# Fused attention and two experts on one Trainium2 core: the reciprocal of a slot's sums ahead of the low halves, and the value products in groups of three

## The chip, the cores and the metric

The kernel runs on one core of a Trainium2 chip. The metric is the device time of one execution in microseconds (us), here the median of three runs.

## What is computed

Attention with a local window and a few global columns, and then two experts, all in float32:

```python
scores = 0.125 * q @ k.T + bias        # kept: column < 8, or 0 <= row - column < 96
a = exp(scores - max(scores))
a = a / (sum(a) + 1e-9)
x = a @ v                               # 4 x 8 heads, 768 rows, 64 columns each
x = ((x @ w1) * (x @ w2)) @ w3 @ w_out  # 3072 rows; 512 -> 1024 -> 1024 -> 512
h = x @ w_in                            # 512 -> 2048
out = (h * cos(h)) @ w_out2             # 2048 -> 512
```

`w3 @ w_out` is formed once, as W.

## The kernel before, in words

The attention is cut into 96 units (`NU`). A unit is 128 rows of one pair of heads; three units (`TPB`) make 384 rows of one pair, and four pairs make a block of 384 rows (`UPB` = 12 units, `NB1` = 8 blocks). A unit passes these steps, each a small function:

- `a_scores`: the products of q and k on TensorE, into `s_ps`.
- `a_max` (L584): VectorE adds the bias and takes each row's maximum, `top`.
- `a_exp` (L595): ScalarE's exponential, one instruction for each of two heads, with the row's sum into `st`.
- `a_norm`: VectorE adds 1e-9 to the sums (L605) and takes the reciprocal (L608); then the 128 x 232 exponentials are scaled by it, on ScalarE (L614) or on GpSimd (L616).
- `a_transpose` and `a_tcopy`: TensorE turns the scaled exponentials into `pt_ps` (L623, L625), ScalarE copies them to `pt` (L633, L638).
- `a_values` (L650): products with v into `x_ps`, one bank for three units.
- `a_out`, after the third unit: ScalarE casts `x_ps` to the high half of `xT` (L664), and VectorE subtracts to get the low half (L665).

Large products use three passes over float32 operands that are split in a high and a low half. From unit 22 on q and k are split as well: `a_split_hi` (L522, ScalarE) and `a_split_lo`, two subtractions on VectorE, `kl` (L529) for k's low halves and `hh` (L532) for q's.

The program has three stages. Each engine works through its own queue in the order in which the code is written; nothing reorders it.

1. **Chunks** (the loop over `chunks`, c = 0 to 15; about 9 to 91 us). Chunk c does a sixteenth of W = w3 @ w_out on TensorE, four products `wmm(0)` to `wmm(3)` (L875). Beside these stand steps of the first 14 units: with n = c - 1, chunk c does the maxima and exponentials of unit n, the scaling of n - 1, the transposes of n - 2 and the value products of n - 3. Between them `decode` takes the next steps of decoding the weights from 64-bit words (ScalarE L343, L344, L406; VectorE L348, L352, L360, L410). The bias tables (L480, L481) are made in chunks 0, 3, 6 and 9. Chunk 15 has an order of its own.
2. **Slots** (the double loop over j and i; about 91 to 607 us). Slot `sl` does the scores, maxima and exponentials of unit n = sl + 14, and the transposes of unit n - 1, beside the first expert's products: in slots i = 0 to 7 of a block `up` a and `up` b, in i = 8 to 11 `down`. The value products and `a_out` stand here in groups of six units, in every sixth slot. For sl < 8 the scaling is on ScalarE, later on GpSimd. `up_mult` (L693), `up_hi` (L697) and `up_lo` (L700) form the operand `ab` of `down`.
3. The second expert, from about 610 us on.

The lines around the change in a slot, on VectorE's queue, are `up_lo`, `a_split_lo`, `a_out`, `a_norm`; in a chunk on TensorE's they are `a_values`, `wmm`, `wmm`, `a_transpose`.

Of the kernel before, what the change touches and what calls it, by code (L numbers as in the profile page):

```python
# [25 lines left out]
WIN = 128 + NPV  # L26
# [3 lines left out]
TPB = TB // 128  # L30
UPB = NPAIR * TPB
NU = NB1 * UPB
# [240 lines left out]
def fused(ctx, tc, a_qk, a_v, a_v0, w3p, wo1p, w1p, w2p, winp, wo2p, out):  # L273
# [210 lines left out]
    def where(n):  # L484
        j, r = divmod(n, UPB)
        p, i = divmod(r, TPB)
        return j, p, i, (TPB * j + i) % (S // 128)
# [109 lines left out]
                bias=top[:, n, e:e + 1], scale=-1.0, accum_out=sts[n][:, 0, e:e + 1],  # L597
            )

    def a_norm(n, on_scalar=False, meanwhile=None):  # L600
        if not 0 <= n < NU:
            return
        w = WIN if where(n)[3] else 128
        st = sts.pop(n)
        nc.vector.tensor_scalar(st[:, 1, :], st[:, 0, :], 1e-9, None, ALU.add)  # L605
        if meanwhile:
            meanwhile()
        nc.vector.reciprocal(out=st[:, 1, :], in_=st[:, 1, :])  # L608
        if meanwhile:
            meanwhile()  # L610
        for e in range(2):
            x = es[n][:, e, :w]
            if on_scalar:
                nc.scalar.activation(x, x, ACTF.Copy, scale=st[:, 1, e:e + 1])  # L614
            else:
                nc.gpsimd.tensor_scalar(x, x, st[:, 1, e:e + 1], 1.0, ALU.mult, ALU.mult)  # L616

    def a_transpose(n):
        if not 0 <= n < NU:
            return  # L620
        e_t, t = es.pop(n), where(n)[3]
        for e in range(2):
            nc.tensor.transpose(pt_ps[:, e, 0, :], e_t[:, e, :128], ident)  # L623
            if t:
                nc.tensor.transpose(pt_ps[:NPV, e, 1, :], e_t[:, e, 128:WIN], ident)  # L625
# [14 lines left out]
    def a_values(n):  # L640
        if not 0 <= n < NU:
            return
        j, p, i, t = where(n)
        if i == 0:
            xps[j, p] = p_mm.tile([128, 512], F32, tag="mm", name="x_ps")[:, :TB]
        x, pt, vt = xps[j, p], pts.pop(n), v_raw.pop(n)
        for c in range(2 if t else 1):
            kk = NPV if c else 128
            for e in range(2):
                nc.tensor.matmul(  # L650
                    x[e * 64:(e + 1) * 64, i * 128:(i + 1) * 128],
                    lhsT=vt[:kk, c, e * 64:(e + 1) * 64], rhs=pt[:kk, e, c, :],
                    start=c == 0, stop=c == (1 if t else 0),
                )

    def a_out(n):
        if not 0 <= n < NU:
            return
        j, p, i, _ = where(n)
        if i != TPB - 1:  # L660
            return
        x = xps.pop((j, p))
        t = xT[j, p] = xts.tile([128, 2, TB], F32R, tag="xT", name="xT")
        nc.scalar.copy(out=t[:, 0, :], in_=x)  # L664
        nc.vector.tensor_tensor(  # L665
            out=t[:, 1, :], in0=x, in1=t[:, 0, :].bitcast(F32), op=ALU.subtract
        )
# [88 lines left out]
    with tc.manual_schedule():  # L756
# [81 lines left out]
        def decode(n):  # L838
            for _ in range(n):
                next(steps_left, None)  # L840
# [16 lines left out]
        for i in range(15):  # L857
            decode(1)
            if i == 0:
                a_load_plain(1, False)  # L860
            elif i == 10:
                a_load_plain(2)
            elif i == 12:
                a_load_v(1)
            if i > 6:
                dists = dists or next(steps_b)
        W_ps = {}
        for c, (h, k) in enumerate(chunks):
            n = c - 1
            own = n if n < LEAD else -9  # L870
            if k == 0:
                W_ps = {m: p_mm.tile([128, 512], F32, tag="mm", name="mm") for m in range(4)}

            def wmm(m):
                nc.tensor.matmul(  # L875
                    W_ps[m], lhsT=wt["w3", c][:, m * 128:(m + 1) * 128], rhs=wt["wo1", k],
                    start=k == 0, stop=k == M1 - 1,
                )
                if k == M1 - 1:
                    t = wt["W", 4 * h + m] = wts.tile(  # L880
                        [128, 2, 512], F32R, tag="Wb" if h else "Wa", name="W", bufs=4
                    )
                    nc.scalar.copy(out=t[:, 0, :], in_=W_ps[m])
                    nc.vector.tensor_tensor(  # L884
                        out=t[:, 1, :], in0=W_ps[m], in1=t[:, 0, :].bitcast(F32), op=ALU.subtract
                    )

            a_load(own + 3)
            a_load_v(n - 1 if n > 2 else -1)
            if c % 3 == 0 and c < 12:  # L890
                bias_heads(*dists, range(2 * c // 3, 2 * c // 3 + 2))
            elif c == 10:
                tp.release()
            if n > 0:
                a_scores(own)
            if n > 0:
                a_load_plain(own + 2)
            a_values(n - 3)
            a_max(own)
            if c == 2 * M1 - 1:  # L900
                a_out(n - 3)
                a_norm(n - 1, True)
                for m in range(4):
                    wmm(m)
            decode(1)
            if c < 2 * M1 - 1:
                a_out(n - 3)
            a_split_hi(own + 2)
            a_exp(own)
            a_split_lo(own + 2)  # L910
            if c < 2 * M1 - 1:
                wmm(0)
                wmm(1)
            a_transpose(n - 2)
            a_tcopy(n - 2)
            decode(1)
            if 1 <= n < 2 * M1 - 2:
                a_norm(n - 1, True, lambda: decode(1))
            else:
                decode(2)  # L920
            decode(2 if c < 8 else {14: 1, 15: 2}.get(c, 3))
            if c < 2 * M1 - 1:
                wmm(2)
                wmm(3)
# [72 lines left out]
        for j in range(NB1):  # L997
            for i in range(UPB):
                sl = j * UPB + i
                n = sl + LEAD  # L1000
                last = j == NB1 - 1
                if last and i == 0:
                    attn.release()
                    x2cA = pool("x2cA", 1)
                    late = pool("late", 1)
                    x2_pool.update({k: x2cA for k in ("B11", "T2", "T1", "T3", "B21", "B22")})
                a_load(n + 3)
                if last:
                    if i == 0:
                        x2_loads(0)  # L1010
                    elif i == 1:
                        r0, r1 = stage_tile(), stage_tile()
                        nc.sync.dma_start(out=r0, in_=x2_cols("B12", 0))
                        x2_now = x2_steps(r0, r1)
                    elif 3 <= i < 9:
                        piece_load(0, i - 3)
                a_scores(n)
                a_load_plain(n + 2)
                group = range(n - 1 - GROUP, n - 1) if (n - 1) % GROUP == 0 and n - 2 < NU else ()
                for u in group:  # L1020
                    if u >= LEAD - 2:
                        a_values(u)
                a_load_v(n)
                a_split_hi(n + 2)
                if 1 <= i <= M1:
                    up_mult(j, i - 1)
                    up_hi(j, i - 1)
                a_max(n)
                decode(2 if sl < 14 else 3)
                if i == 0 and j > 0:  # L1030
                    down_out(j - 1, MO - 1)
                    down_store(j - 1, MO - 1)
                elif i > M1:
                    down_out(j, i - M1 - 1)
                    down_store(j, i - M1 - 1)
                if 1 <= i <= M1:
                    up_lo(j, i - 1)
                a_exp(n)
                a_split_lo(n + 2)
                if i < M1:  # L1040
                    up(j, i, "a")
                    up_copy(j, i)
                else:
                    down(j, i - M1, 0)
                for u in group:
                    if u >= LEAD - 2:
                        a_out(u)
                a_transpose(n - 1)
                a_tcopy(n - 1)
                a_norm(n, sl < 8)  # L1050
                decode(2)
                if last and 2 <= i < 10:
                    some(x2_now, 1)
                if i < M1:
                    up(j, i, "b")
                else:
                    down(j, i - M1, 1)
                if last and 2 <= i < 10:
                    some(x2_now, 1)
# [429 lines left out]
```

## Time and profile before

| what | value |
| --- | --- |
| median of three runs | 1076.93 us (1076.87 to 1077.49) |
| the profiled execution's own time | 1076.14 us |
| its span, first to last instruction | 1074.4 us |
| TensorE (PE) busy | 1056.2 us, 98% |
| VectorE (DVE) busy | 830.7 us, 77% |
| ScalarE (ACT) busy | 730.4 us, 68% |
| GpSimd (POOL) busy | 237.8 us, 22% |
| mean granted TensorE clock | 0.998 |

The span is the stretch that the trace covers; the execution's time is 1.7 us longer. A share of busy time is a mean over stages that have different limits, so the prediction reads stretches and not these shares.

### The profile page before, as it was taken

The numbers are of one execution on the slowest core, as the hardware profiler recorded it, in microseconds if no ns is written. First come the engines' busy times: TensorE is split into PE (matmuls) and PEld (weight loads), VectorE is DVE, ScalarE is ACT, GpSimd is POOL, SyncE is SP. The second block draws the span as 40 slices with busy tenths as digits, with TensorE's granted clock in tenths as the row PEclk, the third lists the DMA queues.
The fourth block names the chain that finished last, engine by engine and source line by source line (L and its number), as shares of the span: only waits on it lengthen the run. The fifth ranks groups of instructions, "written<-read, shape, count | busy, mean of one in ns | idle before, by whom it ended". The sixth has DMA issues, their size and how long they took to land.

```text
span 1074.4 us, 17759 instructions
## 1 busy us (share of the span) xinstructions
PE 1056.2 (98%) x5922; PEld 923.5 (86%) x5922; DVE 830.7 (77%) x1812; ACT 730.4 (68%) x1487; POOL 237.8 (22%) x249
## 2 busy tenths in 40 slices
PE   8999999999999999999999999999999999999997
PEld 5446889999999999999999988888888888888886
DVE  8887777878778787887835378799788899688984
ACT  7998876767677776777733277766478756478652
POOL 0000001111211112111110058600078300288000
PEclk9999999999999999999999999999999999999999
DMA  9864466666756667667444265764866766755553
GB/s 336 292 191 167 159 199 200 199 220 201 241 200 211 221 195 233 203 200 236 158 168 132 84 203 194 245 222 162 298 193 196 243 224 218 250 191 192 173 198 115
DMA packets 88309, 219.25 MB, mean 204 GB/s; under 512 B 9488, under 2 KB 26384, under 8 KB 88208
## 3 DMA queue, kind: packets, MB, share of 16 engines
q1 hardware_dynamic: 87696, 217.44, 60.8%
q8 instruction: 49, 0.80, 0.3%
q10 hardware_dynamic: 512, 0.58, 0.2%
q14 instruction: 52, 0.43, 0.1%
HBM read 176.04 MB, written 41.94 MB: 203 GB/s over the span
## 4 chain that ended last, share of the span: by engine, by line
PE 88%; DVE 6%; ACT 4%; DMA 1%; issue 1%; DVEq 0%; ACTq 0%; SPq 0%
PE h_ps L419 37%; PE mm L419 35%; PE k_ps L419 6%; PE x_ps L650 3%; PE pt_ps L623 2%; PE s_ps L565 2%; PE s_ps L561 1%; PE pt_ps L625 1%; ACT e L614 1%; DMA v<-in_a_v 1%; ACT x L343 1%; DVE w L352 1%; DVE x L352 1%; ACT e L595 1%; DVE x L360 1%
## 5 line engine op out<-in xcount | busy, mean ns | idle before, releaser
L616 POOL TENSOR_SCALAR e<-e,st 128x232 f32<-128x232 f32 x148 | 76.4, 528 | 470.6 <-DVE st L608 232.0
L419 PE MATMUL h_ps<-op,piece 128*128 128x512 f32 x720 | 166.1, 389 | 0.0
L419 PEld LDWEIGHTS h_ps<-op,piece 128*128 128x128 f32 x720 | 135.0, 188 | 28.1
L419 PE MATMUL mm<-ab,W 128*128 128x384 f32 x768 | 146.2, 340 | 0.5 <-DVE ab L700 0.5
L419 PE MATMUL mm<-xT,wB 128*128 128x384 f32 x768 | 145.9, 339 | 0.0
L419 PE MATMUL mm<-xT,wA 128*128 128x384 f32 x768 | 145.0, 338 | 0.0
L419 PE MATMUL h_ps<-T,piece 128*128 128x512 f32 x576 | 138.4, 389 | 0.0
L419 PEld LDWEIGHTS mm<-ab,W 128*128 128x128 f32 x768 | 131.0, 188 | 2.5 <-DVE ab L700 1.2
L419 PEld LDWEIGHTS mm<-xT,wB 128*128 128x128 f32 x768 | 130.9, 188 | 1.8 <-issue 1.1
L419 PEld LDWEIGHTS mm<-xT,wA 128*128 128x128 f32 x768 | 131.0, 188 | 0.6 <-issue 0.6
L419 PEld LDWEIGHTS h_ps<-T,piece 128*128 128x128 f32 x576 | 108.1, 188 | 22.5
L1124 POOL TENSOR_TENSOR gr<-r,gr 128x1024 f32<-128x1024 f32 x21 | 50.5, 2405 | 276.0 <-ACT r L1119 274.5
L419 PE MATMUL h_ps<-B,piece 128*128 128x512 f32 x432 | 105.9, 389 | 0.6 <-ACT x2t L722 0.6
L419 PEld LDWEIGHTS h_ps<-B,piece 128*128 128x128 f32 x432 | 81.0, 188 | 17.7 <-ACT x2t L722 0.9
L595 ACT ACTIVATE e<-e,top 128x232 f32<-128x232 f32 (+1 forms) x192 | 89.2, 466 | 2.2 <-DVE top L584 2.1
L522 ACT CAST hh<-qk 128x720 fp32r<-128x720 f32 x74 | 59.0, 797 | 44.7 <-PE s_ps L565 35.7
L584 DVE CUSTOM_DVE_ANT_0 e<-s_ps,bias 128x232 f32<-128x232 f32 (+1 forms) x192 | 64.9, 375 | 17.0 <-PE s_ps L565 13.7
L419 PE MATMUL k_ps<-op,piece 128*128 128x512 f32 x288 | 67.2, 389 | 0.0
L419 PEld LDWEIGHTS k_ps<-op,piece 128*128 128x128 f32 x288 | 54.1, 188 | 11.2
L1116 ACT ACTIVATE r<-r 128x1024 f32<-128x1024 f32 x48 | 51.0, 1062 | 16.8 <-DVE r L1110 16.8
L875 PE MATMUL mm<-wo,w 128*128 128x512 f32 x128 | 61.3, 606 | 1.1 <-DVE W L884 0.6
L1233 ACT CAST op<-gr 128x512 fp32r<-128x512 f32 x72 | 42.8, 621 | 25.5 <-PE k_ps L419 9.2
(136 smaller groups left out, 1951.6 us busy)
## 6 DMA issues: line engine op xcount, KB each, us to landing
piece<-a_s SPq DMA_DIRECT2D x84, 512.0 KB, 4.0
piece<-o2s SPq DMA_DIRECT2D x84, 512.0 KB, 3.8
qk<-in_a_qk SPq DMA_DIRECT2D x74, 360.0 KB, 3.4
a_s<-ap SPq DMA_DIRECT2D x56, 256.0 KB, 2.6
o2s<-ap SPq DMA_DIRECT2D x56, 256.0 KB, 2.4
v<-in_a_v SPq DMA_DIRECT2D x95, 128.0 KB, 3.4
raw<-in_w3p SPq DMA_DIRECT2D x16, 512.0 KB, 5.0
raw<-in_winp SPq DMA_DIRECT2D x16, 512.0 KB, 3.6
```

The lines of the kernel that those rows point to most:

```text
L352: nc.vector.scalar_tensor_tensor(out=x, in0=raws[key][:, :, 1], scalar=-(1 << 31), in1=x, op0=ALU.bitwise_and, op1=ALU.bitwise_or,)
L419: nc.tensor.matmul(ps, lhsT=l, rhs=r, start=first and i + e == 0, stop=last and i == n - 1 and e == 2, skip_group_check=more,)
L522: nc.scalar.copy(out=hh[n], in_=qk_raw[n])
L565: nc.tensor.matmul(s_ps[n][:, e, :], lhsT=q, rhs=l[:, e * WIN:(e + 1) * WIN], start=False, stop=True,)
L584: nc.vector.tensor_tensor_reduce(out=es[n][:, e, :w], in0=sp[:, e, :w], in1=bias[:, 2 * p + e, :], scale=-0.125, scalar=3.0e38, op0=ALU.ad ...
L595: nc.scalar.activation(es[n][:, e, :w], es[n][:, e, :w], ACTF.Exp, bias=top[:, n, e:e + 1], scale=-1.0, accum_out=sts[n][:, 0, e:e + 1],)
L616: nc.gpsimd.tensor_scalar(x, x, st[:, 1, e:e + 1], 1.0, ALU.mult, ALU.mult)
L650: nc.tensor.matmul(x[e * 64:(e + 1) * 64, i * 128:(i + 1) * 128], lhsT=vt[:kk, c, e * 64:(e + 1) * 64], rhs=pt[:kk, e, c, :], start=c == 0 ...
L875: nc.tensor.matmul(W_ps[m], lhsT=wt["w3", c][:, m * 128:(m + 1) * 128], rhs=wt["wo1", k], start=k == 0, stop=k == M1 - 1,)
L1116: nc.scalar.activation(self.r, self.r, ACTF.Abs)
L1124: engine.tensor_tensor(out=self.h, in0=self.r, in1=self.h, op=ALU.mult)
L1233: nc.scalar.copy(out=t[:, 0, :], in_=x)
```

## The change

Three edits. First, `a_norm` is divided: the sums' addition and reciprocal become `a_stat`, and the scaling stays `a_norm`. In a slot `a_stat(n)` is put directly behind `a_exp(n)`, ahead of `a_split_lo` and `a_out`. Second, in the chunks the value products of three units stand together, in the chunk in which those of the third stood (c = 6, 9 and 12), behind `wmm(0)` and `wmm(1)`; in chunk 15 they stay at its start. Third, in those chunks `a_out` goes behind `a_transpose` and `a_tcopy`.

```diff
-    def a_norm(n, on_scalar=False, meanwhile=None):
+    def a_stat(n, meanwhile=None):
         if not 0 <= n < NU:
             return
-        w = WIN if where(n)[3] else 128
-        st = sts.pop(n)
+        st = sts[n]
         nc.vector.tensor_scalar(st[:, 1, :], st[:, 0, :], 1e-9, None, ALU.add)
         if meanwhile:
             meanwhile()
         nc.vector.reciprocal(out=st[:, 1, :], in_=st[:, 1, :])
         if meanwhile:
             meanwhile()
+
+    def a_norm(n, on_scalar=False):
+        if not 0 <= n < NU:
+            return
+        w = WIN if where(n)[3] else 128
+        st = sts.pop(n)
...
+        def early_values(n):
+            if n >= 0 and n % TPB == TPB - 1:
+                for u in range(n - TPB + 1, n + 1):
+                    a_values(u)
+
...
-            a_values(n - 3)
+            if c == 2 * M1 - 1:
+                early_values(n - 3)
             a_max(own)
             if c == 2 * M1 - 1:
                 a_out(n - 3)
+                a_stat(n - 1)
                 a_norm(n - 1, True)
                 for m in range(4):
                     wmm(m)
             decode(1)
-            if c < 2 * M1 - 1:
-                a_out(n - 3)
             a_split_hi(own + 2)
             a_exp(own)
             a_split_lo(own + 2)
             if c < 2 * M1 - 1:
                 wmm(0)
                 wmm(1)
+                early_values(n - 3)
             a_transpose(n - 2)
             a_tcopy(n - 2)
+            if c < 2 * M1 - 1:
+                a_out(n - 3)
             decode(1)
             if 1 <= n < 2 * M1 - 2:
-                a_norm(n - 1, True, lambda: decode(1))
+                a_stat(n - 1, lambda: decode(1))
+                a_norm(n - 1, True)
...
                 a_exp(n)
+                a_stat(n)
                 a_split_lo(n + 2)
```

What stands in the queues at three places, before and now (line numbers behind L608 move by 5 to 15).

ScalarE in chunk 6, before; `bias` are the tables, `pt` the copy of the transposes, `raw` and `x` a weight in decoding:

```order
L481 ACTIVATE bias_88<-dist 128x232
L664 CAST xT<-x_ps 128x384
L595 ACTIVATE e,st<-e,top 128x232 x2
L638 COPY pt<-pt_ps 128x2x128
L343 ACTIVATE x<-raw 128x512
L344 ACTIVATE raw<-raw 128x512
L614 ACTIVATE e<-e,st 128x232 x2
```

and now:

```order
L481 ACTIVATE bias_88<-dist 128x232
L595 ACTIVATE e,st<-e,top 128x232 x2
L643 COPY pt<-pt_ps 128x2x128
L669 CAST xT<-x_ps 128x384
L343 ACTIVATE x<-raw 128x512
L344 ACTIVATE raw<-raw 128x512
L619 ACTIVATE e<-e,st 128x232 x2
```

The cast for `xT` has moved behind the two exponentials and the copy. VectorE's queue in the chunks has not moved: its subtraction for `xT` (L665, now L670) stands where it stood, ahead of the rest of the decoding and of the sums' reciprocal.

TensorE at the same place, before (`mm` are the products of W):

```order
L650 MATMUL x_ps<-pt,v 64x128 x4
L875 MATMUL mm<-wo_323,w_288 128x512 x2
L623 MATMUL pt_ps<-ident,e 128x128 x2
L875 MATMUL mm<-wo_323,w_288 128x512 x2
L552 MATMUL s_ps<-hh 128x128
```

and now:

```order
L885 MATMUL mm<-wo_323,w_288 128x512 x2
L655 MATMUL x_ps<-pt,v_102 64x128 x2
L655 MATMUL x_ps<-pt,v 64x128 x8
L628 MATMUL pt_ps<-ident,e 128x128 x2
L885 MATMUL mm<-wo_323,w_288 128x512 x2
```

Ten value products, those of units 0 to 2, stand behind two products of W; in chunks 4 and 5, where units 0 and 1 had theirs, there are none.

VectorE in slot sl = 6, before:

```order
L529 TENSOR_TENSOR kl<-qk,hh 128x464
L532 TENSOR_TENSOR hh<-qk,hh 64x256
L605 TENSOR_SCALAR st<-st 128x2
L608 RECIPROCAL st<-st 128x2
L388 TENSOR_TENSOR ap<-x,ap 128x2x128
```

and now:

```order
L604 TENSOR_SCALAR st<-st 128x2
L607 RECIPROCAL st<-st 128x2
L529 TENSOR_TENSOR kl<-qk,hh 128x464
L532 TENSOR_TENSOR hh<-qk,hh 64x256
L388 TENSOR_TENSOR ap<-x,ap 128x2x128
```

The same exchange stands in every slot that splits q and k; where the slot has an `a_out`, its two subtractions go behind the reciprocal too. The queues of ScalarE, GpSimd, TensorE and SyncE in the slots have not moved.

## Rows read from the trace of the kernel before

**Rows 1.** Busy us (instructions) by stretch: PE, PEld, DVE, ACT, POOL, clock, DMA.

```profile
20.00:72.00 52.00, 49.55 (x211) 23.75 (x210) 46.39 (x136) 51.29 (x135) 0.00 (x0) 1.00 0.84 276
59.23:73.50 14.27, 13.51 (x60) 6.77 (x61) 14.27 (x42) 14.27 (x39) 0.00 (x0) 1.00 0.81 266
160.94:204.00 43.06, 43.06 (x294) 42.51 (x295) 33.27 (x100) 30.15 (x79) 7.31 (x15) 1.00 0.60 195
```

**Rows 2.** Waits of PE, 25 to 73.5 us: in total, times, longest.

```profile
PE x_ps L650 <- ACT pt L638: 1.9, 2, 1.1
PE mm L875 <- DVE W L884: 0.6, 1, 0.6
```

**Rows 3.** Timeline of PE, chunk 4: start, us, instruction [idle before <-releaser].

```profile
27.98 0.44 PE L650 MATMUL x_ps<-pt,v 128*64 128x128 f32 x4 [0.81 <-ACT pt L638]
```

**Rows 4.** Timeline of ACT, chunks 4 to 6.

```profile
28.97 0.86 ACT L614 ACTIVATE e<-e,st 128x232 f32<-128x232 f32 x2
...
36.45 0.59 ACT L633 COPY pt<-pt_ps 128x512 f32<-128x512 f32 x1 [0.26 <-PE pt_ps L625]
...
40.75 0.45 ACT L664 CAST xT<-x_ps 128x384 fp32r<-128x384 f32 x1
41.11 0.48 ACT L595 ACTIVATE e<-e,top 128x232 f32<-128x232 f32 x1
...
42.06 0.35 ACT L638 COPY pt<-pt_ps 128x256 f32<-128x256 f32 x1
...
43.45 0.87 ACT L614 ACTIVATE e<-e,st 128x232 f32<-128x232 f32 x2
```

**Rows 5.** Timeline of DVE, chunks 6, 7, 9 and 12.

```profile
41.24 0.56 DVE L665 TENSOR_TENSOR xT<-x_ps,xT 128x384 fp32r<-128x384 f32 x1 [1.93 <-ACT xT L664]
...
42.72 0.16 DVE L608 RECIPROCAL st<-st 128x2 f32<-128x2 f32 x1
...
46.72 1.29 DVE L884 TENSOR_TENSOR W<-mm,W 128x512 fp32r<-128x512 f32 x2 [1.30 <-ACT W L883]
...
58.76 0.56 DVE L665 TENSOR_TENSOR xT<-x_ps,xT 128x384 fp32r<-128x384 f32 x1 [1.26 <-ACT xT L664]
...
72.45 0.55 DVE L665 TENSOR_TENSOR xT<-x_ps,xT 128x384 fp32r<-128x384 f32 x1
...
74.11 0.69 DVE L410 TENSOR_TENSOR wA<-x,wA 128x512 fp32r<-128x512 f32 x1 [0.43 <-ACT wA L406]
```

**Rows 6.** Longest waits of ACT and of DVE, 73.5 to 137 us.

```profile
ACT e L614 <- DVE st L608: 7.5, 10, 1.7
...
DVE x L348 <- ACT x L343: 12.1, 9, 1.6
```

**Rows 7.** Timeline of PE, slots 7 and 8.

```profile
137.41 0.33 PE L623 MATMUL pt_ps<-ident,e 128*128 128x128 f32 x1 [1.03 <-ACT e L614]
...
143.90 0.33 PE L623 MATMUL pt_ps<-ident,e 128*128 128x128 f32 x1 [1.06 <-ACT e L614]
...
146.94 0.62 PE L419 MATMUL mm<-ab,W 128*128 128x384 f32 x2 [0.46 <-DVE ab L700]
```

**Rows 8.** Timeline of ACT, slots 5, 6 and 7.

```profile
129.89 0.87 ACT L614 ACTIVATE e<-e,st 128x232 f32<-128x232 f32 x2 [0.73 <-DVE st L608]
...
136.87 0.87 ACT L614 ACTIVATE e<-e,st 128x232 f32<-128x232 f32 x2 [1.69 <-DVE st L608]
...
143.36 0.87 ACT L614 ACTIVATE e<-e,st 128x232 f32<-128x232 f32 x2 [0.63 <-DVE st L608]
```

**Rows 9.** Timeline of DVE, slot 6.

```profile
135.28 0.64 DVE L529 TENSOR_TENSOR kl<-qk,hh 128x464 fp32r<-128x464 f32 x1
...
135.95 0.42 DVE L532 TENSOR_TENSOR hh<-qk,hh 64x256 fp32r<-64x256 f32 x1
```

**Rows 10.** Timeline of POOL, two slots of the second block.

```profile
175.11 0.73 POOL L616 TENSOR_SCALAR e<-e,st 128x128 f32<-128x128 f32 x2 [4.34 <-DVE st L608]
...
190.41 1.41 POOL L616 TENSOR_SCALAR e<-e,st 128x128 f32<-128x128 f32 x2 [4.68 <-DVE st L608]
```

## The prediction

> **What bounds the kernel.** I read first the windows by engine. From 160.94 to 204 us TensorE (PE) is busy for all of its 43.06 us while VectorE (DVE) has 33.27 and ScalarE (ACT) 30.15 [rows 1]: in the slots TensorE sets the pace, and a change pays only where TensorE still waits. In the chunks it is otherwise [rows 1]. From 20 to 72 us ACT is busy for 51.29 of 52.00 us and TensorE for 49.55, and from 59.23 to 73.50 both DVE and ACT are busy throughout. There ACT, later ACT and DVE together, set the pace.
>
> Next I read who waits for whom. In the chunks TensorE loses 1.9 us to value products whose `pt` ACT has not copied yet and 0.6 us to a product of W [rows 2]. From 73.5 us to the slots' first stretch ACT waits for the sums' reciprocal (7.5 us) and DVE for decoded words from ACT (12.1 us) [rows 6]: two engines in a loop, neither held by TensorE or by a DMA. In the slots with scaling on ACT, TensorE waits for that scaling: 1.03 and 1.06 us, and later 0.46 us for `ab` [rows 7]. The 0.46 us at 146.94 is TensorE's last idle time before 607 us. So only what TensorE gains or loses before about 147 us reaches the end.
>
> **Values in groups of three: they bring nothing.** TensorE's two waits for `pt` go, since the products now come one to two chunks later; one is 0.81 us [rows 3]. But next on TensorE come the transposes of unit 1, and their operand is scaled by ACT from 28.97 to 29.83 [rows 4], later than the values ended (27.98 + 0.44 = 28.42). The wait changes its name. ACT could not have scaled sooner: its idle time in 52 us is 52.00 − 51.29 = 0.71 us. Eight fewer groups of products issue nothing more; no DMA is added or moved, and no queue of SP or POOL is passed. In the loop of ACT and DVE nothing waits for TensorE [rows 6]. Value 0, bounds 0 and the 1.9 + 0.6 = 2.5 us of TensorE's waits (a rival below).
>
> The Trainium skill says, in "Perfetto Trace Analysis", section Optimization Strategy, that one should look for the gaps of the engine that a regime is bound on and remove what blocks it. Applied to TensorE it would give the sum a gain of 2.5 us here; the row says that ACT is full, and by it these are the wrong engine's gaps.
>
> **`a_out` later in its chunk: a loss of 2.0 us.** ACT's cast `xT` (0.45 us, its next instruction starts 0.36 later) now stands behind two exponentials and a copy. These hold ACT for 42.06 − 41.11 = 0.95 us and some 0.25 us (the 0.35 us copy without its overlap), 1.20 together [rows 4]. DVE's subtraction has not moved, and DVE already waits for this cast: 1.93 us in chunk 6, 1.26 in chunk 9, in chunk 12 not at all, the cast being just in time [rows 5]. Behind it on DVE's queue stand the rest of the decoding, the sums' reciprocal, for which ACT's scaling waits, and the next maximum. Chunk by chunk:
> - Chunk 6. ACT's 0.26 us idle at 36.45 goes (it came from the products that are put off), so the cast is 1.20 − 0.26 = 0.94 later and DVE with it. The reciprocal, 42.72 to 42.88, then ends at 43.82 instead; ACT's scaling, at 43.45 before, starts some 0.45 later. DVE's other half us is swallowed by its 1.30 us wait at 46.72. Both leave the chunk +0.45.
> - Chunk 9. DVE starts its subtraction 0.45 + 1.20 = 1.65 later. Both engines are full here [rows 1], so nothing swallows it: DVE +1.65, ACT behind its reciprocals and maxima about +1.25.
> - Chunk 12. The cast is late by 1.25 + 1.20 = 2.45, and since it was just in time before, so is DVE's subtraction. The 0.43 us wait at 74.11 [rows 5] swallows its part: 2.45 − 0.43, about +2.0.
>
> From there the two engines wait only for each other [rows 6], so I carry +2.0 into the slots and to TensorE. Bounds: three delays that add up in full, 3 × 1.20 = 3.6; below, a gain of 0.6 us, nearly all of ACT's 0.71 us idle time. I take 2.0, nearer the upper end, since the stretch from chunk 9 to 12 is full on both engines.
>
> **The reciprocal ahead in the slots: a gain of 2.45 us.** It counts where the scaling is on ACT and q and k are split, in slots 5 to 7 (for slots below 8 without a split or `a_out` the queue does not move). In slot 5 the two subtractions for `xT` no longer stand ahead of the reciprocal, and ACT's 0.73 us wait [rows 8] goes. In slot 6 the low halves `kl` and `hh`, 0.64 + 0.42 = 1.06 us [rows 9], go behind it; ACT's wait there is 1.69, and with slot 5's advance it shrinks to about nothing. So TensorE's 1.03 us at 137.41 goes; so does the 1.06 at 143.90, where ACT's wait was only 0.63 but slot 6 comes earlier. Of the 0.46 for `ab` I leave 0.1. Sum 1.03 + 1.06 + 0.36 = 2.45; bounds 1.03 (the first alone) and 2.55 (all three).
>
> In the other slots the reciprocal gains nothing: TensorE has no idle time that could go. Nor do I charge anything for the later `kl` and `hh`: the scores that read them stand two slots on, and a slot there lasts (190.41 − 175.11) / 3 = 5.1 us [rows 10]. Without that cover each would cost up to 1.06.
>
> GpSimd's scaling moves as well, to beside `kl` and `hh`. The same scaling took 0.73 us at 175.11 and 1.41 at 190.41 [rows 10], the second beside a DVE operation with two operands in SBUF. The 0.68 us more, and as much for DVE, are hidden as long as DVE has idle time.
>
> The Trainium skill states, in "SBUF — State Buffer", section Who interferes with whom, that such operations of DVE and GpSimd's share a port and that one holds the other off completely, which speaks against this change; the two durations agree with it in direction.
>
> **Sum.** The profiled execution took 1076.14 us. 1076.14 + 2.0 − 2.45 = 1075.69. The median of the runs stands 0.79 above that execution, so the forecast is 1076.5. Its own range: 1076.14 − 0.6 − 2.55 + 0.79 = 1073.8, and 1076.14 + 3.6 − 1.03 + 0.79 = 1079.5. I take 0.2%, 2.15 us, as what a measurement can tell from no change: faster is below 1074.8, slower above 1079.1.
>
> **Rivals.**
> - A. TensorE sets the pace in the chunks after all, its waits there close, and the cast's delay is hidden: 1076.14 − 2.5 − 2.45 + 0.79 = 1072.0. For it: TensorE is busy for 95% of 20 to 72 us. Against: ACT for 98.6%. It is also the result of the skill's rule on gaps. Chance 0.09.
> - B. The chunks lose nothing: DVE's later start is swallowed by its other waits, 12.1 us of them behind chunk 12 [rows 6]. 1076.14 − 2.45 + 0.79 = 1074.5, or 1073.9 with a gain of 0.6. Against: those waits are for ACT, which is itself late by the reciprocal. Chance 0.08.
> - C. Slower: DVE becomes the bound of the `up` slots. The sums' addition now stands at the head of its queue and must wait for ACT's exponentials, with `kl`, `hh` and `xT` behind it, 1.06 us of work that could run meanwhile before. DVE's idle time in the third window is 43.06 − 33.27 = 9.79 us over 43.06 / 5.1 = 8.4 slots, 1.17 us a slot. It decides once the wait and the contention use up that 1.17; each 0.1 us beyond, in the 56 `up` slots behind slot 8, costs 5.6 us: 1075.7 + 5.6 + 0.8 = 1082.1. Against: the room is just above 1.06. Chance 0.08.
> - D. The reorder doesn't do what it says in the slots: ACT's exponentials, not the low halves, are what the reciprocal waits for. Then only the chunks' loss stays: 1076.14 + 2.0 + 0.79 = 1078.9. Against: in slot 6 the low halves run on DVE directly ahead of the sums [rows 9]. Chance 0.05.
>
> **Chances.** Forecast 0.70 (0.08 faster, 0.52 within, 0.10 slower by its own range). A and 0.06 of B are faster, 0.02 of B within; C and 0.02 of D slower, 0.03 of D within. Faster 0.08 + 0.09 + 0.06 = 0.23; within 0.57; slower 0.10 + 0.08 + 0.02 = 0.20. The range, 1073.4 to 1079.6, takes in the forecast's own, B and D, and leaves out A and C, 0.17, and a little of B's and the forecast's tails.
>
> **What would show it.** Right in the chunks: DVE's waits for the cast grow from 1.93, 1.26 and 0 us to about 2.9, 2.5 and 1.2; ACT idles ahead of a scaling one chunk on; TensorE's waits for `pt` become waits of its transposes for the scaling; and the slots' first scores come 2.0 us later. Wrong, towards A or B: the slots start at the same time or sooner. Right in the slots: the waits at 137.41 and 143.90 are gone, TensorE is without a gap from slot 8 on, and its last product of the slots ends where it did, by half a us or less. Wrong, towards C: idle time of TensorE behind 150 us with `ab` or `s_ps` late from DVE. Towards D: the reciprocals of slots 6 and 7 wait for ACT's exponentials and the 1.0 us waits stay.

## The result and the profile after

| | median | ratio to the kernel before | 95% interval |
| --- | --- | --- | --- |
| before | 1076.90 us | | |
| changed | 1091.30 us | 1.0130 | 1.0117 to 1.0142 |

The changed kernel is 14.4 us slower, and outside the predicted range. Two marks on TensorE's timeline divide the loss: the first scores of the slots and the first product of the second expert. Before:

```profile
90.67 1.05 PE L552 MATMUL s_ps<-hh 64*128 64x232 f32 x8
...
610.37 1.66 PE L419 MATMUL h_ps<-B,piece 128*128 128x512 f32 x6 [0.61 <-ACT x2t L722]
```

After:

```profile
93.00 1.05 PE L552 MATMUL s_ps<-hh 64*128 64x232 f32 x8
...
626.09 1.55 PE L419 MATMUL h_ps<-B,piece 128*128 128x512 f32 x6
```

The chunks lost 93.00 − 90.67 = 2.33 us, where 2.0 was forecast. The slots, from one mark to the other, took 533.09 us instead of 519.70. Behind the second mark nothing more is lost.

**Chunks.** On VectorE's timeline the three subtractions for `xT`, which answer to [rows 5], now wait as the prediction said (about 2.9, 2.5 and 1.2 us):

```profile
42.20 0.56 DVE L670 TENSOR_TENSOR xT<-x_ps,xT 128x384 fp32r<-128x384 f32 x1 [3.15 <-ACT xT L669]
...
60.46 0.56 DVE L670 TENSOR_TENSOR xT<-x_ps,xT 128x384 fp32r<-128x384 f32 x1 [2.46 <-ACT xT L669]
...
75.30 0.56 DVE L670 TENSOR_TENSOR xT<-x_ps,xT 128x384 fp32r<-128x384 f32 x1 [1.15 <-ACT xT L669]
```

TensorE's waits for `pt` [rows 2] have gone, and its transposes wait for the scaling instead: 3.7 us in 3 waits from 25 to 73.5 us.

**Slots 4 to 8.** TensorE's two waits at 137.41 and 143.90 [rows 7] are gone and the 0.46 for `ab` has stayed (0.45 at 146.60). By the start of each slot's scores the lag of 2.33 us turns into a lead of 0.33 at 147 us: a gain of 2.66, where 2.45 was forecast.

**Slots behind 200 us.** The lead holds until 208 us. Then the lag grows in steps, slot by slot, of 0.1 to 1.5 us: 0.38 at 218 us, 3.9 at 293, 7.4 at 357, 11.1 at 478, 15.9 at the last slots. That is 16.2 us, and it is this that makes the kernel slower. TensorE had no idle time between 147 and 607 us before. Now, in the list of its waits from 150 to 610 us:

```profile
PE pt_ps L628 <- POOL e L621: 4.9, 15, 0.7
PE mm L419 <- DVE ab L705: 4.7, 5, 1.4
PE mm L419 <- DVE xT L670: 0.5, 1, 0.5
```

These are 10.1 of the 16.2 us. The rest doesn't show as idle time: where TensorE was stopped, the first instructions behind the stop are listed as longer (a transpose 0.33 us instead of 0.27) and overlap less, so that a stop costs more than its idle time. At 343.17 us, for one, 0.88 us are listed and the lag grows by 1.33.

The windows, which answer to [rows 1]:

```profile
20.00:72.00 52.00, 48.16 (x192) 22.50 (x190) 44.69 (x133) 50.36 (x131) 0.00 (x0) 1.00 0.80 269
59.23:73.50 14.27, 12.38 (x57) 5.84 (x55) 13.04 (x38) 13.50 (x35) 0.00 (x0) 1.00 0.75 245
160.94:204.00 43.06, 43.06 (x296) 42.51 (x295) 33.62 (x96) 30.38 (x79) 8.96 (x16) 1.00 0.62 203
```

In the chunks every engine now has idle time, ScalarE too. In the slots GpSimd's busy time has grown from 7.31 us for 15 entries to 8.96 for 16, and VectorE's by 0.35 us, while TensorE is still full here: this window lies ahead of the first step.

What VectorE and ScalarE wait for, 150 to 610 us, before:

```profile
DVE st L605 <- ACT e L595: 11.7, 13, 2.9
...
ACT ab L697 <- DVE a_sb L693: 23.5, 27, 2.6
```

and after:

```profile
DVE st L604 <- ACT e L595: 38.0, 35, 3.9
...
ACT ab L702 <- DVE a_sb L698: 50.3, 43, 2.8
```

The sums' addition has become the head of VectorE's queue while ScalarE is still at the exponentials. ScalarE in turn waits twice as long for VectorE's product `a_sb`, from which it makes the high half of `ab`. The groups by line and shape, 150 to 610 us, show a second thing. Before:

```profile
L529 DVE TENSOR_TENSOR kl<-qk,hh 128x464 fp32r<-128x464 f32 x71 | 45.1, 635 | 0.0
L532 DVE TENSOR_TENSOR hh<-qk,hh 64x256 fp32r<-64x256 f32 x71 | 30.0, 422 | 1.0
...
L616 POOL TENSOR_SCALAR e<-e,st 128x232 f32<-128x232 f32 x122 | 64.6, 541 | 279.9 <-DVE st L608 187.4 <-ACT pt L633 41.8 <-PE mm L419 18.6
```

After:

```profile
L529 DVE TENSOR_TENSOR kl<-qk,hh 128x464 fp32r<-128x464 f32 x71 | 44.1, 622 | 0.0
L532 DVE TENSOR_TENSOR hh<-qk,hh 64x256 fp32r<-64x256 f32 x71 | 40.3, 567 | 1.0
...
L621 POOL TENSOR_SCALAR e<-e,st 128x232 f32<-128x232 f32 x122 | 77.0, 642 | 284.7 <-DVE st L607 163.1 <-ACT pt L638 72.5 <-PE s_ps L565 12.8
```

q's low half takes 0.567 us instead of 0.422 and each scaling 0.642 instead of 0.541; they now run beside each other, and the experiments e4 and e9 below show that this is why.

**One step, read closely.** Before, VectorE in a slot whose scores start at 273.96 us:

```profile
273.73 0.17 DVE L608 RECIPROCAL st<-st 128x2 f32<-128x2 f32 x1
273.81 0.67 DVE L352 SCALAR_TENSOR_TENSOR x<-raw,x 128x512 int32<-128x512 int32 x1
274.52 0.83 DVE L360 CUSTOM_DVE_ANT_0 x<-raw,x 128x1024 uint16<-128x1024 uint16 x1
275.28 0.54 DVE L693 TENSOR_TENSOR a_sb<-mm,a_sb 128x384 f32<-128x384 f32 x1
```

After, in the same slot, whose scores start at 275.98:

```profile
276.00 0.17 DVE L607 RECIPROCAL st<-st 128x2 f32<-128x2 f32 x1
276.08 0.62 DVE L529 TENSOR_TENSOR kl<-qk,hh 128x464 fp32r<-128x464 f32 x1
276.71 0.58 DVE L532 TENSOR_TENSOR hh<-qk,hh 64x256 fp32r<-64x256 f32 x1
277.33 0.83 DVE L352 SCALAR_TENSOR_TENSOR x<-raw,x 128x512 int32<-128x512 int32 x1
278.20 0.69 DVE L360 CUSTOM_DVE_ANT_0 x<-raw,x 128x1024 uint16<-128x1024 uint16 x1
278.81 0.55 DVE L698 TENSOR_TENSOR a_sb<-mm,a_sb 128x384 f32<-128x384 f32 x1
...
281.33 0.43 DVE L388 TENSOR_TENSOR ap<-x,ap 128x256 fp32r<-128x256 f32 x1 [1.34 <-ACT ap L386]
281.68 0.55 DVE L705 TENSOR_TENSOR ab<-a_sb,ab 128x384 fp32r<-128x384 f32 x1
```

Relative to the slot's scores the reciprocal is 0.25 us later than before, although it has moved ahead: VectorE enters this slot late. `kl` and `hh` then follow, and the product `a_sb` comes 2.83 us behind the scores instead of 1.32. ScalarE waits for it; VectorE waits for ScalarE (1.34 us, at a piece `ap` of a decoded weight), and the low half of `ab` stands behind that piece; TensorE waits for that low half, on its timeline:

```profile
282.28 0.61 PE L419 MATMUL mm<-ab,W 128*128 128x384 f32 x2 [1.43 <-DVE ab L705]
```

The 1.5 us by which `a_sb` is late and this 1.43 us are about the same. GpSimd's scaling beside it began at 276.36, 0.34 us ahead of the end of `kl`, and took 1.27 us for two instructions. Before, about half of these pairs took 0.89 to 0.91 us (the one at 280.29 us, for example), others more: 1.59 us in this very slot, beside the decoding. After, nearly all take 1.27 or 1.28. In the Trainium skill, "SBUF — State Buffer", section Who interferes with whom, the one that issues second is held off until the first has finished; the 0.38 us above 0.89 agree with the 0.34. For `hh`, which comes next on VectorE's queue, a hold for the whole of a scaling (some 0.45 us, half of 0.89) doesn't come out: it grew by 0.16 us.

The other and slightly larger part of TensorE's waits is for the scaling itself (4.9 us). One of these waits, back to its cause:

```profile
341.88 0.17 DVE L604 TENSOR_SCALAR st<-st 128x2 f32<-128x2 f32 x1 [1.76 <-ACT e L595]
```

```profile
342.44 1.27 POOL L621 TENSOR_SCALAR e<-e,st 128x232 f32<-128x232 f32 x2 [5.63 <-DVE st L607]
```

```profile
343.17 0.33 PE L628 MATMUL pt_ps<-ident,e 128*128 128x128 f32 x1 [0.72 <-POOL e L621]
```

The sums come late, since the exponentials do (the second one of the unit ends 1.99 us behind the slot's first score product; in the kernel before it was 0.13 us), and the scaling that follows takes 1.27 us instead of 1.14.

### The profile page after: what moved, and what is told of

Same layout as the page of the kernel before. It is cut to its first block, busy times and chain, and to the rows that moved or that the text cites. A ratio compares the mean times of both kernels' runs of the same rounds, so it can differ in the third digit from the quotient of the medians.

```text
span 1089.6 us, 17745 instructions
## 1 busy us (share of the span) xinstructions
PE 1061.0 (97%) x5922; PEld 922.1 (85%) x5922; DVE 845.6 (78%) x1812; ACT 730.2 (67%) x1487; POOL 252.9 (23%) x249
## 5 line engine op out<-in xcount | busy, mean ns | idle before, releaser
L621 POOL TENSOR_SCALAR e<-e,st 128x232 f32<-128x232 f32 x148 | 91.4, 628 | 472.7 <-ACT pt L638 238.7
L419 PEld LDWEIGHTS h_ps<-B,piece 128*128 128x128 f32 x432 | 81.1, 188 | 16.7
L702 ACT CAST ab<-a_sb 128x384 fp32r<-128x384 f32 x64 | 32.8, 513 | 55.9 <-DVE a_sb L698 55.8
L1131 ACT ACTIVATE r<-r 128x1024 f32<-128x1024 f32 x48 | 51.0, 1062 | 16.7 <-DVE r L1125 16.7
```

The lines of the kernel that those rows point to most:

```text
L419: nc.tensor.matmul(ps, lhsT=l, rhs=r, start=first and i + e == 0, stop=last and i == n - 1 and e == 2, skip_group_check=more,)
L702: nc.scalar.copy(out=ab[m][:, 0, :], in_=ab_f[m])
L1131: nc.scalar.activation(self.r, self.r, ACTF.Abs)
```

## The experiments

Two theories on the 16.2 us: **W**, VectorE waits at the head of its queue for the exponentials, and the low halves no longer run in that time; **K**, scaling and low halves lengthen each other. Rivals beside these: the chunks set it off; the earlier reciprocal by itself; the buffers of q and k. "Slots" below is the time from the slots' first scores to the second expert's first product in the profiled execution; it leaves out what the chunks do. It comes from one execution of each kernel, and the runs of a kernel spread (the changed kernel's from 1088.18 to 1091.52 us, those of e11 by 4.5 us), so the shares worked out from it below are good to one or two us.

| run | median us | ratio (interval) | slots, us |
| --- | --- | --- | --- |
| before | 1076.90 | | 519.70 |
| changed | 1091.30 | 1.0130 (1.0117 to 1.0142) | 533.09 |
| e1 chunks alone | 1078.68 | 1.0017 (1.0008 to 1.0027) | 520.16 |
| e2 slots alone | 1089.31 | 1.0115 (1.0098 to 1.0132) | 532.79 |
| e3 slots 0 to 7 and chunks | 1075.72 | 0.9993 (0.9983 to 1.0003) | 516.41 |
| e4 addition alone ahead | 1082.44 | 1.0056 (1.0040 to 1.0073) | 522.83 |
| e5 slots 0 to 7, old chunks | 1074.09 | 0.9978 (0.9968 to 0.9987) | 517.66 |
| e6 sums between `kl` and `hh` | 1079.05 | 1.0025 (1.0014 to 1.0036) | 520.63 |
| e7 values by three, old place | 1072.80 | 0.9967 (0.9955 to 0.9979) | 516.75 |
| e8 subtraction late | 1072.89 | 0.9970 (0.9959 to 0.9981) | 516.51 |
| e9 scaling held | 1087.01 | 1.0096 (1.0081 to 1.0111) | 527.14 |
| e10 GpSimd beside, no wait | 1076.57 | 1.0000 (0.9990 to 1.0010) | 517.27 |
| e11 down slots alone | 1081.04 | 1.0046 (1.0031 to 1.0061) | 521.41 |
| e12 three q/k buffers | 1091.24 | 1.0139 (1.0122 to 1.0156) | 531.35 |
| e13 low halves at the maximum | 1082.65 | 1.0061 (1.0044 to 1.0077) | 522.21 |

### The two parts apart (e1, e2)

e1 takes the early reciprocal out of the slots again:

```diff
                 a_exp(n)
-                a_stat(n)
                 a_split_lo(n + 2)
...
+                a_stat(n)
                 a_norm(n, sl < 8)
```

> Only the chunks' part of the change (values in groups of three, a_out later); in every slot the reciprocal stands behind the low halves as before. Theory W (the changed kernel loses in the slots, where the sums' addition now waits for ScalarE's exponentials at the head of VectorE's queue): the chunks' loss of 2.3 us, the first slot's scores at 93.0 instead of 90.67, is carried to the end and nothing else is lost: 1079.2. Rival (the later chunks set off the slots' waits): 1086 or more, with waits of TensorE for ab or e behind 200 us.

Measured: 1078.68, 2.0 us above the 1076.7 of the kernel before beside it, and first scores at 92.98. The chunks' loss is carried whole and sets off nothing.

e2 puts the chunks back and leaves the slots as changed:

```diff
                 wmm(1)
-                early_values(n - 3)
             a_transpose(n - 2)
             a_tcopy(n - 2)
-            if c < 2 * M1 - 1:
-                a_out(n - 3)
```

(with `a_values(n - 3)` ahead of the maximum and `a_out(n - 3)` behind the first decoding step, as they were)

> Only the slots' part (reciprocal ahead of the low halves in every slot), the chunks as before. Theory W: 2.3 us less than the changed kernel's 1091.3, so 1089.0, with some 16 us of steps in the slots behind 200 us. Rival (chunks set them off): 1074.5, the slots' 2.45 us gained and nothing lost.

Measured: 1089.31. The parts add up: 2.0 and 12.6 us make 14.6, and the whole change cost 14.4.

### The early slots alone (e3)

```diff
                 a_exp(n)
-                a_stat(n)
+                if sl < 8:
+                    a_stat(n)
                 a_split_lo(n + 2)
...
+                if sl >= 8:
+                    a_stat(n)
                 a_norm(n, sl < 8)
```

> The changed kernel, but the reciprocal stands ahead of the low halves only in slots 0 to 7, where ScalarE scales; from slot 8 on it stands behind them as before. Theory W and theory K (GpSimd's scaling and the low halves lengthen each other) both: 1076.9 + 2.33 - 2.67 = 1076.6, TensorE without a gap from 150 to 610 us. If the early slots' order shifts the later slots into waits: above 1080.

Measured: 1075.72, and TensorE has no wait between 147 and 610 us. This kernel is the one that the prediction's sum describes (1076.5): the sum was right for the slots that it had counted. The loss belongs to slots 8 on.

### Wait or contention (e4, e9, e10)

e4 puts only the sums' addition ahead from slot 8 on, so that VectorE waits as in the changed kernel, while the scaling starts behind the low halves (edit shown against e3):

```diff
                 a_exp(n)
-                if sl < 8:
-                    a_stat(n)
+                if sl < 8:
+                    a_stat(n)
+                else:
+                    a_add(n)
                 a_split_lo(n + 2)
...
-                    a_stat(n)
+                    a_stat(n, added=True)
                 a_norm(n, sl < 8)
```

> As the run with the first slots alone, but from slot 8 on the sums' addition (not the reciprocal) stands ahead of the low halves: VectorE waits there for the exponentials as in the changed kernel, and GpSimd's scaling starts behind the low halves as before. Theory W (the wait at the head of the queue): most of the 16 us stays, 1086 to 1095. Theory K (contention of scaling and low halves): near the run with the first slots alone, 1076 to 1079, VectorE's wait for the exponentials near 38 us and yet no loss.

Measured: 1082.44, between what either theory gave. VectorE's wait and GpSimd's group, 150 to 610 us:

```profile
DVE st L604 <- ACT e L595: 40.4, 36, 3.7
```

```profile
L628 POOL TENSOR_SCALAR e<-e,st 128x232 f32<-128x232 f32 x123 | 64.5, 536 | 290.1 <-DVE st L614 189.8 <-PE mm L419 35.6 <-PE s_ps L565 28.3
```

The wait is all there (40.4 us beside 38.0), the contention is gone (0.536 us). The slots take 522.83 − 516.41 = 6.4 us more than in e3, of the changed kernel's 533.09 − 516.41 = 16.7. So the wait alone costs 6.4; the other 10.3 come when the reciprocal, and with it the scaling, is ahead too. (By the medians it is 6.7 and 8.9.)

e9 is the changed kernel with the scaling held until the low halves are done:

```diff
+        if not on_scalar and n + 2 in hh:
+            nc.gpsimd.tensor_scalar(
+                held[64:65, :], hh[n + 2][64:65, :1].bitcast(F32), 1.0, 1.0, ALU.mult, ALU.mult
+            )
         for e in range(2):
             x = es[n][:, e, :w]
```

> The changed kernel, but ahead of each of GpSimd's scalings stands a copy of one column of q's new low half on GpSimd, so that the scaling begins only when the low halves are done; VectorE's queue is the changed kernel's, reciprocal early. Theory K (of the 16 us, 6 are the wait for the exponentials and 10 the contention of scaling and low halves): near the run with the addition alone ahead, 1080 to 1084, with the low half of q back at 0.42 us from 0.57. Rival (the place of the reciprocal, or what it moves on VectorE, costs the 10 us): 1088 or more.

Measured: 1087.01, between the two, slots 527.14: 6.0 us of the 10.3 went with the contention (`hh` back at 0.422 us), 4.3 did not. TensorE's waits for `ab` fell from 4.7 to 0.6 us, as in e4; those for the scaling only from 4.9 to 3.3 (e4: 2.2). Since the added copy holds GpSimd for 0.33 us in each slot ahead of the scaling, the 4.3 can be its price or the reciprocal's; this run doesn't tell.

e10 is e3 with work for GpSimd, of the scaling's size, beside the low halves, and no wait:

```diff
                 if 1 <= i <= M1:
                     up_lo(j, i - 1)
+                    if sl >= 8:
+                        for _ in range(2):
+                            nc.gpsimd.tensor_scalar(
+                                spare, ab[i - 1][:, 1, :WIN].bitcast(F32), 1.0, 1.0,
+                                ALU.mult, ALU.mult,
+                            )
```

> As the run with the first slots alone, and in the up slots from slot 9 on two instructions of GpSimd of the scaling's size, which read the operand ab and write a spare tile, run beside VectorE's low halves: contention without the wait at the head of the queue. Theory (only both together use up VectorE's spare time): VectorE's low halves take 0.1 to 0.3 us longer in a slot, and the time stays within 2 us of 1075.7. Rival (the contention alone costs the 10 us that the wait doesn't explain): 1083 or more.

Measured: 1076.57, slots 0.9 us longer than in e3. Its groups, 150 to 610 us:

```profile
L532 DVE TENSOR_TENSOR hh<-qk,hh 64x256 fp32r<-64x256 f32 x71 | 33.8, 476 | 1.0
...
L604 DVE TENSOR_SCALAR st<-st 128x2 f32<-128x2 f32 x73 | 14.9, 204 | 12.9 <-ACT e L595 11.4
```

Some 0.09 us more a slot for VectorE, in `hh` and the addition, cost next to nothing as long as it doesn't wait (11.4 us, 11.7 before). It is a weaker contention than the changed kernel's (0.476 beside 0.567 us), and `hh` grew by less than the 0.1 to 0.3 us expected, so it bounds the price from one side only.

### Cover for the exponentials (e6, e13)

e6 puts `kl` ahead of the sums and only `hh` behind them, from slot 8 on:

```diff
             out=kl[n], in0=r[:, 256:], in1=t[:, 256:].bitcast(F32), op=ALU.subtract
         )
+        if between is not None:
+            a_stat(between)
         nc.vector.tensor_tensor(
...
-                a_stat(n)
-                a_split_lo(n + 2)
+                if sl < 8:
+                    a_stat(n)
+                    a_split_lo(n + 2)
+                else:
+                    a_split_lo(n + 2, n)
```

> As the changed kernel, but from slot 8 on k's low half stands ahead of the sums and only q's behind the reciprocal. Theory (wait and contention use up the same spare time of VectorE): k's 0.64 us runs during the exponentials, so the wait for them shrinks from 38 us to 15 to 25, q's low half still meets GpSimd's scaling (0.50 to 0.58 us instead of 0.42): between the run with the first slots alone (1075.7) and the changed kernel, 1077 to 1083. Rival (it's the earlier scaling by itself): 1087 or more.

Measured: 1079.05, slots 4.2 us above e3. Its wait, 150 to 610 us, and GpSimd's group:

```profile
DVE st L608 <- ACT e L599: 23.3, 27, 3.7
```

```profile
L625 POOL TENSOR_SCALAR e<-e,st 128x232 f32<-128x232 f32 x122 | 74.7, 623 | 275.7 <-DVE st L611 150.5 <-ACT pt L642 67.3 <-PE s_ps L569 23.6
```

The scaling is nearly as slow as in the changed kernel (0.623 beside 0.642 us), yet three quarters of the 16.7 us are gone, with 0.64 us of work put back into the time of the exponentials. `hh` was not lengthened (0.423 us); that part of the expectation failed.

e13 (with e12's three buffers) puts both low halves directly behind the next unit's maximum, and leaves the reciprocal directly behind `up_lo`:

```diff
                 a_max(n)
+                if sl > 8:
+                    a_split_lo(n + 1)
                 decode(2 if sl < 14 else 3)
...
                 a_stat(n)
-                a_split_lo(n + 2)
+                if sl < 8:
+                    a_split_lo(n + 2)
```

> As the run with three buffers (1091.2), but from slot 9 on the low halves of unit n + 1 stand directly behind the maximum of unit n, ahead of decoding and up_lo; the reciprocal stays directly behind up_lo. Theory (what costs is that the low halves no longer run while ScalarE does the exponentials, and that they stand ahead of the next slot's product and maximum): VectorE's wait for the exponentials falls from 38 us to 20 or less and the time to 1074 to 1080. Rival (the earlier reciprocal and scaling cost by themselves): 1085 or more.

Measured: 1082.65, outside both. VectorE's wait is 26.8 us, not 20, and the slots are 5.8 us above e3, so 10.9 of the 16.7 are back. The early reciprocal by itself is refuted as the main cause; some 6 us stay, about as much as in e4, whose addition also stands directly behind `up_lo` and waits. Some of it is a price of e13's own order: its scores wait 1.1 us for `hh`, which they do in none of the other runs.

### Which slots (e11)

```diff
+                soon = sl < 8 or not 1 <= i <= M1
                 a_exp(n)
-                a_stat(n)
+                if soon:
+                    a_stat(n)
                 a_split_lo(n + 2)
...
+                if not soon:
+                    a_stat(n)
                 a_norm(n, sl < 8)
```

> As the run with the first slots alone, but from slot 8 on the reciprocal is ahead in the slots without up_mult and up_lo (4 of 12 in a block), and behind in the other 8. Theory (VectorE has no room only where it also makes ab): 1075.7 to 1078. Rival (the loss is spread over all slots, a third of 16.7 us): 1080 or more.

Measured: 1081.04; the rival was right. With 4 of 12 slots in the new order the slots lose 5.0 us, near a third of 16.7: the loss is not a matter of the slots that make `ab`. The longest single loss of this run, 1.9 us of lag, is at a wait of the transposes for GpSimd's scaling (1.41 us, at 451.71 us), behind a VectorE wait of 3.74 us for ScalarE's cast `ap`, a piece of a decoded weight. That wait goes on to a DMA; this run, and the same place before:

```profile
445.90 0.41 ACT L386 CAST ap<-x 128x256 fp32r<-128x256 f32 x1 [3.99 <-DMA o2s<-ap]
```

```profile
440.60 0.41 ACT L386 CAST ap<-x 128x256 fp32r<-128x256 f32 x1 [2.18 <-DMA o2s<-ap]
```

ScalarE waits for the store of an earlier piece, and that store needs the piece's low half from VectorE (L388). So at this place the loop runs over VectorE, SyncE's DMA queue and ScalarE, which is a path of its own beside `ab`. No run gives `ap` another buffer; why a slot without `a_sb` and `ab` has no room either wasn't tried further.

### The buffers of q and k (e12)

The raw q and k of a unit have two buffers, and the low halves are their last readers. In the changed kernel SyncE's queue waits for them ahead of the loads:

```profile
SPq L496 <- DVE hh L532: 35.8, 23, 1.8
```

(before: 9.0 us, 8 times, and 12.5 us, 10 times, put down to the sums' addition, which stood right behind `hh`). e12 is the changed kernel with a third buffer:

```diff
-        t = attn.tile([128, 768], F32, tag="qk", name="qk", bufs=2)[:, :QK_W]
+        t = attn.tile([128, QK_W], F32, tag="qk", name="qk", bufs=3)[:, :QK_W]
```

> The changed kernel with three buffers for the raw q and k in place of two (other tiles cut to the width that is used, to make room). Behind the change the low halves, the last readers of such a buffer, come later, and ScalarE's waits for the load of q and k grow from 3.2 to 10.1 us between 150 and 610 us. Theory (the loss is VectorE's queue: the wait for the exponentials, and contention): these waits fall to 3 us or less and the time stays within 3 us of 1091.3. Rival (the later release of the buffers delays the loads and, through ScalarE, everything): 1085 or less.

Measured: 1091.24, as the changed kernel. SyncE's waits for `hh` are gone, but ScalarE's waits for the loads stay, against the expectation, at 10.0 us: they are not the buffers' doing. The buffers cost nothing here.

### The chunks (e5, e7, e8)

e5 is e3 with the chunks of the kernel before. e7 adds to e5 the grouping alone, at the old place:

```diff
-            a_values(n - 3)
+            if n >= 3 and (n - 3) % TPB == TPB - 1:
+                for u in range(n - 3 - TPB + 1, n - 2):
+                    a_values(u)
             a_max(own)
```

e8 is e3, changed chunks included, with VectorE's subtraction behind the sums' reciprocal:

```diff
+            late_low = []
             if c < 2 * M1 - 1:
-                a_out(n - 3)
+                a_out(n - 3, late_low)
             decode(1)
...
             else:
                 decode(2)
+            for low in late_low:
+                low()
```

> The reciprocal ahead of the low halves in slots 0 to 7 only, and the chunks as in the kernel before. If the chunks' loss and the first slots' gain are independent: the run with the changed chunks less its 2.3 us, 1075.7 - 2.3 = 1073.4, or 1076.9 - 2.67 = 1074.2 from the kernel before. If the later chunks' loss was swallowed in the slots: 1075.7.

> As the run before in this list, but in the chunks the values of three units stand together at the old place (ahead of the maximum), with a_out where it was. Theory (ScalarE and VectorE set the pace in the chunks): TensorE's two waits for pt, 1.9 us, go, and the time stays within 0.5 us of the run before. Rival (TensorE's waits cost time): 1.5 to 2 us less than it.

> As the first of this list, but with the changed chunks (values by three, the cast for xT behind exponentials and copy), and VectorE's subtraction for xT moved behind the sums' reciprocal and two steps of decoding. Theory (the loss is VectorE waiting for the late cast with the decoding and the reciprocal behind it): the loss of 2.3 us goes, within 0.6 us of the first of this list, and the first slot's scores come at 90.2 to 91.2 us. Rival (the later cast delays ScalarE or TensorE itself): 2 us or more above it, scores at 93.

Measured: 1074.09, 1072.80 and 1072.89. e5 is faster than the kernel before beyond its interval: the first slots' gain is real. e8 against e3 (0.9970 and 0.9993, intervals apart) shows what the chunks' loss was: with the same late cast, but the subtraction behind the reciprocal and the decoding, the slots' first scores come at 90.69 us instead of 92.99. e7 and e8 are a little faster than expected (within 0.5 and 0.6 us of e5). e7 is 1.3 us below e5: their intervals against the kernel before overlap, but of e7's six runs (1072.27 to 1073.68) four lie below all nine of e5's (1073.32 to 1075.01), so a gain is likely. In the profiled executions e7's first scores come 0.49 us sooner (90.52 against 91.01), but e2 and the kernel before, with e5's chunks, stand at 90.72 and 90.67; most of the rest lies at the slots' end, where e5, like the kernel before, waits 0.61 us for `x2t` and e7 does not. How much of the 1.3 the grouping itself gives is not shown. e7 and e8 beat both kernels, by 0.33% and 0.30%, and can't be told from each other.

## Why the prediction was wrong

- **Values by three, 0.** Right in the mechanism: the waits for `pt` went and turned into waits for the scaling, as said. The size is probably too small: e7 is 1.3 us below e5, within the bound of 2.5 that was kept.
- **`a_out` later, +2.0.** Right in mechanism: the three waits are 3.15, 2.46 and 1.15 us, and e8 shows that what was queued behind the subtraction was the cost. The +2.33 at the first scores and the +2.0 in e1 are the two chunk edits together; if the grouping gains something there, `a_out` cost that much more (against e7, which has the grouping too, e3's first scores come 2.47 us later), and that the sum is so close would be luck in part.
- **The reciprocal in slots 5 to 7, −2.45.** Right in the sum, −2.66, but not term by term: the wait for `ab` stayed, and the two waits for the scaling, 1.03 and 1.06 us of idle time, gave back 1.4 and 1.3 us of lag.
- **The reciprocal from slot 8 on, 0.** This is the step that failed: "Nor do I charge anything for the later `kl` and `hh`: the scores that read them stand two slots on". The scores were indeed never late. But the low halves had two other parts: they were VectorE's work while ScalarE did the exponentials, and they now stand ahead of the next product `a_sb` and the next maximum. In their place came a longer wait of VectorE (11.7 to 38.0 us) and a late product `a_sb` (by 1.5 us in the slot read above), and with these the loop between VectorE and ScalarE: 16.2 us in all, as waits of TensorE for `ab` and for the scaling. The wait alone makes 6.4 (e4). With it falls the sentence that only what TensorE gains or loses before about 147 us reaches the end: it held for the old order.
- **"Hidden as long as DVE has idle time".** The 1.17 us a slot were a mean, and idle time of an engine that waits for another in a loop isn't free room. The contention, which costs at most 1 us by itself in e10's weaker form, took 6.0 us on top of the wait (e9).
- **Rival C** named this mechanism and its place, with a chance of 0.08. It was priced at 0.1 us beyond the room in each `up` slot, 5.6 us. Measured are 16.2 us, and not in `up` slots alone (e11).

What stays open: 4.3 us between e9 and e4, and what the slots without `ab` lack; the stores of `ap` are a lead that no run tested.

## What to carry to other kernels

Ahead of moving work on an in-order queue, ask what it covered: work that stands just ahead of an instruction that needs another engine's result may be all that fills the time until that result is there. Count the room left on an engine by slot and by what its idle time waits for, not as a mean, and look behind the moved work as well as at its readers. An order that helps where one engine scales (slots 0 to 7) can harm where another does; it can be given to those slots alone.

## What was not expected of the hardware

In the profiled executions of four runs (e9, e10, e11, e13) the changed chunks, with the same instructions, reached the slots 0.9 to 1.7 us later than 93.0 us. TensorE's wait for the scaling is the same in the changed kernel:

```profile
63.00 0.33 PE L628 MATMUL pt_ps<-ident,e 128*128 128x128 f32 x1 [1.89 <-ACT e L619]
...
63.66 1.88 PE L885 MATMUL mm<-wo,w 128*128 128x512 f32 x4
```

and in e9, one of the four:

```profile
62.90 0.33 PE L634 MATMUL pt_ps<-ident,e 128*128 128x128 f32 x1 [1.90 <-ACT e L625]
...
63.56 3.42 PE L891 MATMUL mm<-wo,w 128*128 128x512 f32 x4
```

Four products of W took 3.42 us instead of 1.88. The windows of e9 show the granted clock there (the column behind the five engines):

```profile
62.00:63.00 1.00, 0.10 (x1) 0.10 (x2) 1.00 (x4) 0.64 (x2) 0.00 (x0) 1.00 0.41 66
...
64.00:65.00 1.00, 1.00 (x2) 0.34 (x1) 1.00 (x6) 0.67 (x2) 0.00 (x0) 0.50 0.93 254
```

0.50 is the lower level, 1.2 GHz; it was granted behind the wait of 1.90 us and was back at 1.00 (2.4 GHz) by 68 us. In the changed kernel the same wait of 1.89 us left the clock at 1.00, and in e10 a wait of 1.89 us was followed by the fall. The runs don't show what decides between the two; it is why the table compares the slots from their first scores. In the ten runs of e1 the mean granted clock goes with the time: the four at 0.997 took 1079.28 to 1079.91 us, the six at 0.998 and 0.999 took 1077.62 to 1078.71. That the same fall makes this difference is likely but not shown, since only one of the ten, at 0.998, has a trace.
